# Windowed attention and routed experts on one core: row sums from a column of ones, copies moved to ScalarE, keys and queries laid out by group

## The chip, the core and the metric

The kernel runs on one core of a Trainium2 chip. A core has five engines with an instruction queue each, worked off in order: TensorE (PE in the profile; its weight loads are PEld), VectorE (DVE), ScalarE (ACT), GpSimd (POOL) and SyncE (SP), which here only issues transfers (DMA). Tiles lie in SBUF; PE writes into the eight banks of PSUM. The metric is the time of one execution on the device in microseconds (us): the median of several runs.

## What is computed

```python
B, H, S, D = 8, 8, 576, 64            # q, k, v: [B, H, S, D], fp32
scores = matmul(q, k.T) / 8           # per batch and head
rel = pos[:, None] - pos[None, :]
scores = where((rel >= 0) & (rel < 64), scores, -1e9)
attn = softmax(scores)
x = (attn @ v).transpose(0, 2, 1, 3).reshape(4608, 512)
logits = x @ w_gate + modality_bias[modality_id]      # 8 experts
e = argmax(logits, axis=1)
gate = softmax(logits)[e]
out[n] = gate[n] * (relu(x[n] @ w1[e]) @ w2[e])       # w1: 512x1024, w2: 1024x512 per expert
```

A query sees its own and the 63 keys before it. Each of the 4608 tokens goes through one expert.

## The kernel before

**Blocks and steps.** The sequence of each batch is cut in blocks of 64 positions, 72 in all; two neighbouring blocks are a pair `p`, 36 in all. A loop over steps `s` works in a pipeline: in step `s` the scores of pair `s` are computed, the probabilities of pair `s-1` are transposed, pair `s-2` is multiplied with its values, and pair `s-3` is routed. The order of each engine's queue is the order in which the loop emits its instructions. Two pairs are a group `G` of four blocks.

**One step, in the order of emission.** `values(s-2)` and `values_out(s-2)`: PE multiplies the transposed probabilities `pT` with the values, DVE multiplies the result by the reciprocals `rs` of the rows' sums into `xa`. `logits(s-3)` on PE and an addition on DVE into `lg`. `scores(s)`: 32 small PE matmuls into the two banks `sp`. `minima(s)`: eight custom DVE instructions add the mask and take each row's minimum of the negated scores (`ss`, `mn`). `swap_v(s-1)` and `probs_t(s-1)`. `exps(s)`: eight ACT instructions, in three portions, raise `e` to the shifted scores and sum each row into `sm`. `x_t(s-2)`: transposition for the logits. Then come two halves of the next group's heads: in an even step both halves of its keys, in an odd step both halves of its queries (`heads_t` on PE, `heads_out` on DVE or ACT). In odd steps from 5 on the routing of an older group (`route2`, `route3`) ends with an index `idx` on DVE and two scatters on POOL, which write rows `xa` to the scratch tensor `xs_scratch` in DRAM.

**Keys and queries.** `kT` and `qT` hold two groups, `[P, HP, RING, W64]`: head pair, then ring place of the block, then position; each group is a slice of four places in every head pair. Scores of a block read its own keys and those of the block ahead of it.

**Values.** `vo[p]` holds the pair's values by position. `ve[p]` holds the same two blocks shifted by one: its lower half is the lower half of `vo[p]` (copied by POOL), its upper half is the upper half of `vo[p-1]`, the neighbour (copied by DVE, `L502`). One matmul with `vo` and one with `ve` give a block its 128 keys.

**Experts.** The weights of two experts are loaded in pieces, split in a high and a low part (`Whi` on ACT, `Wlo` on DVE); a piece per step from step 3 on. From step `FIRST` = 12 on, the expert matmuls of rows scattered earlier fill gaps of the attention steps on PE; after step 39 they alone remain. `EARLY` fixes which groups' rows are taken when. Small DVE instructions that plan these loads stand in a queue of their own and are emitted a few at a time by `tick`.

**Banks.** `turn_bank` hands out banks for transposes in turn; up to step 10 there are five of them (two `tp`, `em`, `y0`, `y1`).

**The start.** Before step 0, SP and ACT issue the loads of group 0's keys and queries; ACT then issues those of the modality numbers (`mod_i`), the bias rows and the gate weights. `first_pair(0)` transposes and copies the first two blocks' heads; `first_pair(1)`, the other two blocks of group 0, follows the scores of step 0. A transposition of the modality numbers stands on PE between the heads of step 0 and the scores of step 1; from it POOL makes `bias_sel`.

## Time and profile before

| | |
|---|---|
| three runs | 647.55, 648.55, 649.33 us; median 648.55 |
| the profiled execution | 648.28 us, span 646.4 us |
| busy in the span | PE 620.0 us (96%), DVE 367.7 (57%), ACT 299.4 (46%), POOL 137.4 (21%) |
| granted clock of PE, mean | 0.996 |
| DMA | 88.07 MB, mean 136 GB/s; 116746 of 138885 packets under 512 B |
| minima of step 0 | start at 14.30 us |
| minima of step 12 | start at 86.23 us |

The span runs from the first to the last instruction; the profiled execution's time is 1.9 us longer. In a row of the timeline stand start, duration, engine, line of the kernel, instruction, tiles, shape, count, and in square brackets how long the engine sat idle ahead of it and what ended that. Instructions of one engine overlap, so the distance of two starts can be smaller than a duration. A row of the windows view gives, for a stretch, the busy time of each engine with its count of instructions, the granted clock of PE, the busy share of the 16 DMA engines and what they moved. A row of the waits view reads: who waited, for whom, us in total, times, the longest.

### The profile page before, as it was taken

The page shows a single profiled execution, that of the slowest core. Times are in us where ns is not written, and L with a number is a line of the kernel's source. Part 1 is how long each engine was busy: PE and PEld are TensorE (multiplying, and loading weights), DVE is VectorE, ACT ScalarE, POOL GpSimd, SP SyncE. Part 2 cuts the span into 40 slices and gives each one's busy share as a digit, 9 for nine tenths or more (in the row PEclk, how much of TensorE's full clock was granted, in tenths as well). Part 3 has the DMA queues.
Part 4 walks back from the last instruction along what each step waited for, and adds up shares of the span by engine and source line. Part 5 has one row for each costly group of instructions (what it writes and reads, how often), then busy time and mean ns, then how long its engine had stood idle before and what let it go on. Part 6 is the DMA issues. An engine that isn't in the chain of part 4 may idle for free.

```text
span 646.4 us, 17286 instructions
## 1 busy us (share of the span) xinstructions
PE 620.0 (96%) x6508; PEld 554.6 (86%) x6509; DVE 367.7 (57%) x1494; ACT 299.4 (46%) x932; POOL 137.4 (21%) x314
## 2 busy tenths in 40 slices
PE   6888889999999999999999999999999999999996
PEld 4677779898989888889998898899898999989986
DVE  2889967777767686766655365122214524757611
ACT  2789875756565646555544111111113513555411
POOL 4315330232142212320322220011011101101102
PEclk9999989999999999999999999999999999999999
DMA  9988975764876754553412124421041732677300
GB/s 164 195 186 216 212 197 132 196 161 120 181 171 153 159 144 103 144 133 82 132 51 83 50 99 171 157 67 66 23 173 45 236 113 85 218 247 227 120 1 36
DMA packets 138885, 88.07 MB, mean 136 GB/s; under 512 B 116746, under 2 KB 116784, under 8 KB 138672
## 3 DMA queue, kind: packets, MB, share of 16 engines
q1 hardware_dynamic: 130112, 67.44, 42.2%
q0 software_dynamic: 5856, 18.92, 7.8%
q10 hardware_dynamic: 2832, 0.59, 0.6%
q8 instruction: 52, 0.85, 0.6%
q14 instruction: 33, 0.27, 0.2%
HBM read 67.49 MB, written 23.91 MB: 141 GB/s over the span
## 4 chain that ended last, share of the span: by engine, by line
PE 50%; DVE 0%; ACT 0%; issue 0%; POOL 0%; POOLq 0%; ACTq 0%
PE y L301 22%; PE em L279 12%; PE sp L279 10%; PE tp L439 1%; PE y L352 1%; PE av L615 1%; PE em L254 1%; PE tp L254 1%; PE sp L327 0%; PE em L327 0%; PE tp L640 0%; PE sp L563 0%; DVE xa L623 0%; ACT ss L589 0%; DVE hl L288 0%
## 5 line engine op out<-in xcount | busy, mean ns | idle before, releaser
L301 PE MATMUL y<-Whi,hh 128*128 128x512 f32 x288 | 118.7, 412 | 0.0
L301 PE MATMUL y<-Wlo,hh 128*128 128x512 f32 x288 | 112.9, 392 | 0.0
L301 PE MATMUL y<-Whi,hl 128*128 128x512 f32 x288 | 112.8, 392 | 0.0
L589 ACT ACTIVATE ss<-ss,mn 128x128 f32<-128x128 f32 x288 | 112.5, 397 | 0.0
L279 PE MATMUL em<-xh,Whi 128*128 128x256 f32 x400 | 103.5, 293 | 1.2 <-ACT xh L192 0.7
L279 PE MATMUL em<-xh,Wlo 128*128 128x256 f32 x400 | 98.5, 280 | 0.0
L288 DVE SCALAR_TENSOR_TENSOR hl<-em,hh 128x512 fp32r<-128x512 f32 x50 | 34.5, 690 | 92.9 <-ACT hh L287 91.3
L312 POOL DMA_INDIRECT out_dram<-y,id x36 | 37.3, 1036 | 224.6 <-DVE y L309 145.9
L279 PEld LDWEIGHTS em<-xh,Whi 128*128 128x128 f32 x400 | 75.9, 190 | 2.6 <-ACT xh L192 0.9
L279 PEld LDWEIGHTS em<-xh,Wlo 128*128 128x128 f32 x400 | 75.8, 190 | 0.9
L287 ACT ACTIVATE hh<-em 128x512 fp32r<-128x512 f32 x50 | 29.6, 592 | 93.3 <-PE em L279 89.4
L577 DVE CUSTOM_DVE_ANT_0 ss<-sp,masks 128x128 f32<-128x128 f32 x288 | 63.5, 286 | 13.4 <-PE sp L563 13.4
L598 ACT COPY pT<-tp 128x512 f32<-128x512 f32 x58 | 32.2, 589 | 78.0 <-PE tp L439 78.0
L301 PEld LDWEIGHTS y<-Whi,hl 128*128 128x128 f32 x288 | 54.1, 188 | 12.3
L279 PE MATMUL em<-xl,Whi 128*128 128x256 f32 x400 | 63.4, 281 | 0.0
L301 PEld LDWEIGHTS y<-Whi,hh 128*128 128x128 f32 x288 | 54.1, 188 | 7.5
L301 PEld LDWEIGHTS y<-Wlo,hh 128*128 128x128 f32 x288 | 54.3, 188 | 7.1
L589 ACT ACTIVATION_READ_ACCUMULATOR ss<-ss,mn 128x1 f32 x288 | 55.8, 194 | 0.0
L716 POOL DMA_INDIRECT xs_scratch<-xa,idx x36 | 36.3, 1007 | 89.1 <-DVE lm L659 26.9
L279 PEld LDWEIGHTS em<-xl,Whi 128*128 128x128 f32 x400 | 54.2, 189 | 0.0
L288 DVE SCALAR_TENSOR_TENSOR hl<-sp,hh 128x512 fp32r<-128x512 f32 x22 | 15.2, 692 | 61.1 <-ACT hh L287 61.1
L615 PEld LDWEIGHTS av<-ve,pT 128*64 128x64 f32 x576 | 36.4, 138 | 15.2 <-issue 7.4
(242 smaller groups left out, 1243.6 us busy)
## 6 DMA issues: line engine op xcount, KB each, us to landing
xt<-xs_scratch SPq DMA_DIRECT2D x18, 514.0 KB, 4.0
vo<-in_v_dram SPq DMA_DIRECT2D x32, 256.0 KB, 4.1
y<-in_moe_w_dram SPq DMA_DIRECT2D x32, 256.0 KB, 4.0
vo<-in_moe_w_dram SPq DMA_DIRECT2D x24, 256.0 KB, 3.5
ss<-in_moe_w_dram SPq DMA_DIRECT2D x24, 256.0 KB, 3.8
qk<-in_k_dram SPq DMA_DIRECT2D x18, 256.0 KB, 5.5
qk<-in_q_dram SPq DMA_DIRECT2D x18, 256.0 KB, 4.9
xs_scratch<-xs_scratch SPq DMA_DIRECT2D x8, 514.0 KB, 6.0
```

The lines of the kernel that those rows point to most:

```text
L254: nc.tensor.transpose(out=tp[:, n * P:(n + 1) * P].bitcast(F32R), in_=xt[:, t, c * P:(c + 1) * P].bitcast(F32R), identity=ident_r)
L279: nc.tensor.matmul(out=hb[:, i * TP:(i + 1) * TP], lhsT=w[buf][:, c0:c0 + P], rhs=x[:, c * TP:(c + 1) * TP], start=(n == 0), stop=(n == le ...
L287: nc.scalar.activation(out=hh, in_=hb, func=AF.Relu),
L288: nc.vector.scalar_tensor_tensor(out=hl, in0=hb, scalar=0.0, in1=hh.bitcast(F32), op0=ALU.max, op1=ALU.subtract)))
L301: nc.tensor.matmul(out=sl["y", t], lhsT=h[:, i * TP + t * P:i * TP + (t + 1) * P], rhs=w[buf][:, c0:c0 + DM], start=(k == 0 and n == 0), s ...
L312: ins = nc.gpsimd.indirect_dma_start(out=out, out_offset=bass.IndirectOffsetOnAxis(ap=sl["id"][:, t:t + 1], axis=0), in_=y, in_offset=None ...
L352: nc.tensor.matmul(out=yp[:, cols], lhsT=sl["h", n][lo][:, c * P:(c + 1) * P], rhs=w[buf][:, c0 + cols.start:c0 + cols.stop], start=(m == ...
L577: nc.vector.tensor_tensor_reduce(out=ss[a][:, hp, :], in0=sp[a][:, hp * P:(hp + 1) * P], in1=mask, scale=-1.0 / 8.0, scalar=3.0e38, op0=AL ...
L589: nc.scalar.activation(out=ss[a][:, hp, :], in_=ss[a][:, hp, :], func=AF.Exp, bias=mn[:, h:h + 1], scale=-1.0, accum_out=sm[:, h:h + 1])
L598: nc.scalar.copy(out=pT, in_=pp)
L615: nc.tensor.matmul(out=av[c * W64:(c + 1) * W64, 2 * hp + a], lhsT=pT[:, i:i + W64], rhs=(vo if c else ve)[p][:, 2 * hp + a, :], start=Tru ...
L716: ins = nc.gpsimd.indirect_dma_start(out=xs, out_offset=bass.IndirectOffsetOnAxis(ap=idx[:, j:j + 1], axis=0), in_=xg[j], in_offset=None)
```

## The change

Six things change together.

1. Row sums. For pairs below `FIRST` the exponentials no longer sum their rows. `vo` and `ve` become fixed tiles with a 65th column per head that holds ones, and the values' matmul takes 65 columns; its last one is the row's sum. The result then needs two banks, `av` and `y1`, which leaves four for `turn_bank`. `values_out` adds 1e-9 on DVE (two instructions) where POOL did, and multiplies in two halves.
2. ScalarE copies. The neighbour's values in `ve` are copied by ACT for pairs below `FIRST`, at the start of a step (`swap_upper`); the second half of the queries' heads is copied by ACT in steps before `FIRST`.
3. `kT` and `qT` are laid out by group: group, head pair, place, position.
4. The first heads: transposes are ordered by the two loads they need (even and odd positions), and each copy of `first_pair(0)` is divided between DVE and ACT. `first_pair(1)` comes after five of step 0's exponentials, so on DVE after the minima. ACT issues the loads of modality numbers, bias rows and gate weights after the first copies.
5. The write of padding rows to `xs_scratch` (SP) moves from the end of step 2 to the end of step 5.
6. Two small tiles take the buffers of others (`wm` those of `lm`, `tgt` those of `wn`).

```diff
+    kT = att.tile([P, 2 * HP * GBLK, W64], F32, name="kT")
+    qT = att.tile([P, 2 * HP * GBLK, W64], F32, name="qT")
+    def place(g, hp):
+        a, j = divmod(g, GBLK)
+        return (a * HP + hp) * GBLK + j
+    vos = [att.tile([P, H, D + 1], F32, name=f"vo{i}") for i in range(3)]
+    ves = [att.tile([P, H, D + 1], F32, name=f"ve{i}") for i in range(2)]
...
-        if s < FIRST - 1 and i % 5 > 1:
-            return ps_m.tile([P, 512], F32, name=("em", "y0", "y1")[i % 5 - 2])
+        if s < FIRST - 1 and i % 4 > 1:
+            return ps_m.tile([P, 512], F32, name=("em", "y0")[i % 4 - 2])
...
-            nc.vector.tensor_copy(out=e[W64:P], in_=vo[p - 1][W64:P])
         nc.gpsimd.tensor_copy(out=e[0:W64], in_=vo[p][0:W64])
+    def swap_upper(p):
+        ve[p] = ves[p % 2]
+        if p > 0:
+            copy = nc.scalar.copy if p < FIRST else nc.vector.tensor_copy
+            copy(out=ve[p][W64:P], in_=vo[p - 1][W64:P])
...
-                bias=mn[:, h:h + 1], scale=-1.0, accum_out=sm[:, h:h + 1])
+                bias=mn[:, h:h + 1], scale=-1.0, accum_out=sm[:, h:h + 1] if p >= FIRST else None)
...
+        if p < FIRST:
+            for i in range(2):
+                nc.vector.tensor_scalar(
+                    out=rs[:, i * HP:(i + 1) * HP], in0=av[i][:, :, D], scalar1=1e-9, scalar2=None, op0=ALU.add)
         nc.vector.reciprocal(out=rs, in_=rs)
...
-    first_pair(0)
+    first_pair(0, (both, both))
+    nc.scalar.dma_start(out=mod_i, in_=mod_id.bitcast(I32).rearrange("(g x) -> g x", x=2 * P))
...
+        if 1 <= s <= NPR:
+            swap_upper(s - 1)
         if 2 <= s < NPR + 2:
             values(s - 2)
...
-                first_pair(1)
             minima(s)
...
+        if s == 0:
+            first_pair(1, (both[:1], both[1:]))
...
-            heads_out(tp, G, *heads[1], nc.scalar.copy if heads[1] == K1 else nc.vector.tensor_copy)
+            heads_out(tp, G, *heads[1], nc.scalar.copy if heads[1] == K1 or s < FIRST else nc.vector.tensor_copy)
...
-        if s == 2:
+        if s == 5:
             nc.sync.dma_start(out=xs_blk[DUMMY:DUMMY + 2].rearrange("b p c -> p b c"), in_=padrow)
```

How this moves instructions shows at three places. A row of these lists is one instruction in its engine's order: line, operation, output and inputs, shape, what its queue waits for, and a count where it is repeated. The first is ACT's queue from the last exponentials of step 5 to the probabilities' copies `pT` of step 6; before:

```order
L589 ACTIVATE ss,sm<-ss,mn 128x128 [waits DVE_49] x6
L111 CAST Whi_65<-y 128x512 [waits DMAHW1_49]
L598 COPY pT<-tp 128x512 [waits PE_49]
L598 COPY pT<-em 128x512 [waits PE_49]
L589 ACTIVATE ss,sm<-ss,mn 128x128 [waits DVE_49,Pool_49]
```

and of the change:

```order
L613 ACTIVATE ss<-ss,mn 128x128 [waits DVE_49] x6
L552 COPY qT<-em 128x2x2x128 [waits PE_49]
L111 CAST Whi_65<-y 128x512 [waits DMAHW0_49]
L517 COPY ve_111<-vo_108 64x520 [waits DMAHW2_49]
L622 COPY pT<-tp 128x512 [waits PE_49,Activation_49] x2
```

ACT has two copies more between the exponentials of an odd step and the `pT` of the next, and its exponentials write no `sm` and wait no longer for POOL.

The second is DVE at the end of an odd step; before, from the second half of the queries' heads to the addition of the logits:

```order
L539 COPY qT<-y_942 128x2x2x128 [waits PE_49]
L702 TENSOR_REDUCE se<-ex 128x2 [waits Activation_49]
L703 TENSOR_TENSOR tgt<-tgt,oh 128x16 [waits DVE_49]
L704 TENSOR_SCALAR se<-se 128x2 [waits DVE_49]
L706 TENSOR_REDUCE dst<-tgt 128x2 [waits DVE_49]
L710 RECIPROCAL xa_101<-se 128x1 [waits DVE_49]
L710 RECIPROCAL xa_102<-se 128x1
L728 CAST idx<-dst 128x2 [waits DVE_49]
L116 TENSOR_TENSOR Wlo_66<-y,Whi_65 128x512 [waits DMAHW0_49,Activation_49]
L621 RECIPROCAL rs<-rs 128x8 [waits Pool_49]
L623 TENSOR_TENSOR xa_105<-av,rs 128x512 [waits DVE_49,PE_49]
L645 TENSOR_TENSOR lg<-tp,bias_sel 128x8 [waits PE_49]
```

and of the change, where `wn` is the former `tgt`:

```order
L744 TENSOR_TENSOR wn<-wn,oh 128x16 [waits DVE_49]
L745 TENSOR_SCALAR se<-se 128x2 [waits DVE_49]
L747 TENSOR_REDUCE dst<-wn 128x2 [waits DVE_49]
L751 RECIPROCAL xa_101<-se 128x1 [waits DVE_49]
L751 RECIPROCAL xa_102<-se 128x1
L769 CAST idx<-dst 128x2 [waits DVE_49]
L116 TENSOR_TENSOR Wlo_66<-y,Whi_65 128x512 [waits DMAHW7_49,Activation_49]
L659 TENSOR_SCALAR rs<-av 128x4 [waits PE_49]
L659 TENSOR_SCALAR rs<-y_978 128x4 [waits PE_49]
L661 RECIPROCAL rs<-rs 128x8 [waits DVE_49]
L664 TENSOR_TENSOR xa_105<-av,rs 128x256 [waits DVE_49]
L664 TENSOR_TENSOR xa_105<-y_978,rs 128x256
```

The heads' copy has left DVE; the two instructions for `rs` and `xa` have become five.

The third is SP around the weights' piece and the values of step 6; before:

```order
L524 DMA Whi_64<-in_q_dram 64x8x64 [waits DMAHW5_49]
L100 ISA
L100 DMA y<-in_moe_w_dram 128x512 [waits DMAHW6_49]
L489 DMA vo<-in_v_dram 128x8x64 [waits DVE_49,DMAHW7_49,PE_49,Pool_49]
L104 ISA
```

and of the change:

```order
L538 DMA Whi_64<-in_q_dram 64x8x64 [waits DMAHW4_49]
L100 ISA
L100 DMA y<-in_moe_w_dram 128x512 [waits DMAHW5_49]
L1076 DMA xs_scratch<-xt 128x2x514 [waits DMAHW6_49,DMASW1_49,DMASW0_49]
L500 DMA vo_107<-in_v_dram 128x8x64 [waits PE_49,DMAHW7_49,Activation_49,Pool_49]
```

The write of the padding rows stands ahead of `vo` and waits for the two scatters of group 0 (`DMASW0`, `DMASW1`).

More of the change, by code (lines that the diff above doesn't have):

```diff
@@ L695, in route3 @@
         xg = [st.pop((GB * G + j, "xa")) for j in range(GB)]
-        tgt = small.tile(sh3, F32, name="tgt")
+        tgt = small.tile(sh3, F32, name="wn")
         nc.vector.tensor_tensor(
@@ L860, in tile_window_attn_moe @@
                     pattern=[[1, W64]], channel_multiplier=-1)
+    for t in vos + ves:
+        nc.gpsimd.memset(t[:, :, D:], 1.0)
     nc.gpsimd.memset(first_oh, 0.0)
@@ L926, in select_bias, with first_pair @@
                 nc.gpsimd.tensor_tensor(out=bias_sel, in0=bias_sel, in1=dst, op=ALU.add)
-    def first_pair(i):
-        for nm in "kq":
-            first_heads(nm, i, turn_bank(0), nc.vector.tensor_copy if nm == "k" else nc.scalar.copy)
-    first_pair(0)
+    both = nc.vector.tensor_copy, nc.scalar.copy
+    def first_pair(i, copies):
+        tps = [turn_bank(0) for _ in "kq"]
+        for t in range(2):
+            for nm, tp in zip("kq", tps):
+                first_heads_t(nm, i, t, tp)
+        for nm, tp, c in zip("kq", tps, copies):
+            first_heads_out(nm, i, tp, c)
+    first_pair(0, (both, both))
+    nc.scalar.dma_start(out=mod_i, in_=mod_id.bitcast(I32).rearrange("(g x) -> g x", x=2 * P))
+    nc.scalar.dma_start(
+        out=brow, in_=mod_bias.rearrange("(o m) e -> o m e", o=1).broadcast_to([P, 2, E]))
+    nc.scalar.dma_start(out=wg, in_=w_gate.rearrange("(c p) e -> p c e", p=P))
     def weights(s):
```

95 lines of the change are left out of this document (55 added, 40 removed).

## The prediction

> **What bounds the kernel now.** I read the busy time of each engine by stretch first, because shares over the whole span (PE 96%) mix stages with different limits. I cut the stretches at the starts of DVE's score minima (`L577`), which mark the attention steps.
>
> ```profile
> core 0: us, PE busy (x) PEld busy (x) DVE busy (x) ACT busy (x) POOL busy (x), PEclk, DMA share, GB/s
> ...
> 14.30:25.31 11.01, 8.36 (x129) 6.25 (x127) 8.28 (x53) 8.87 (x38) 5.43 (x11) 1.00 1.19 203
> ...
> 48.73:72.19 23.46, 20.75 (x410) 18.35 (x408) 22.53 (x122) 21.90 (x85) 9.20 (x17) 1.00 0.88 212
> 72.19:86.23 14.04, 10.45 (x200) 8.62 (x199) 12.65 (x74) 10.72 (x42) 4.36 (x9) 1.00 0.76 180
> 86.23:100.00 13.77, 11.82 (x143) 10.66 (x142) 8.95 (x45) 8.56 (x28) 4.87 (x10) 0.88 0.92 229
> 100.00:627.00 527.00, 525.23 (x5075) 474.32 (x5074) 288.72 (x1084) 224.69 (x656) 98.33 (x206) 1.00 0.46 129
> ```
>
> From 100 us on PE is busy 525.23 of 527.00 us. Nothing that the change takes from DVE or ACT can count there; PE's work there stays. The change can only move the whole of it forward, by making steps 0 to 11 end earlier. In the four steps from 48.73 to 72.19 DVE is busy 22.53 of 23.46 us (96%), ACT 93%, PE 88%: DVE sets the pace, ACT is just behind it. So the second view is DVE's timeline over one odd step (minima of step 7 to minima of step 8); the columns are start, duration, instruction.
>
> ```profile
> 54.67 0.28 DVE L577 CUSTOM_DVE_ANT_0 ss<-sp,masks 128x128 f32<-128x128 f32 x1
> ...
> 56.47 0.42 DVE L502 COPY ve<-vo 64x512 f32<-64x512 f32 x1
> 56.93 0.69 DVE L539 COPY qT<-tp 128x512 f32<-128x512 f32 x1
> ...
> 57.74 0.68 DVE L539 COPY qT<-em 128x512 f32<-128x512 f32 x1
> 58.34 0.16 DVE L702 TENSOR_REDUCE se<-ex 128x2 f32<-128x16 f32 x1
> ...
> 59.54 0.20 DVE L621 RECIPROCAL rs<-rs 128x8 f32<-128x8 f32 x1
> 59.82 0.69 DVE L623 TENSOR_TENSOR xa<-av,rs 128x512 f32<-128x512 f32 x1
> 60.43 0.15 DVE L645 TENSOR_TENSOR lg<-y,bias_sel 128x8 f32<-128x8 f32 x1
> 60.50 0.28 DVE L577 CUSTOM_DVE_ANT_0 ss<-sp,masks 128x128 f32<-128x128 f32 x1
> ```
>
> No row carries an idle mark: DVE goes from one instruction to the next. Durations overlap, so I price an instruction by start to start: the neighbours' copy `ve` 0.46 us, a heads' copy 0.60 (57.74 to 58.34), `xa` 0.61, the dependent step from `rs` to `xa` 0.28. Earlier steps do have waits, and the waits view gives their sum:
>
> ```profile
> DVE ss L577 <- PE sp L563: 5.3, 6, 2.2
> 42.88 0.29 DVE L577 CUSTOM_DVE_ANT_0 ss<-sp,masks 128x128 f32<-128x128 f32 x1 [1.25 <-PE sp L563]
> 42.27 0.45 PE L563 MATMUL sp<-kT,qT 64*64 64x128 f32 x8 [0.97 <-ACT kT L539]
> 48.73 0.28 DVE L577 CUSTOM_DVE_ANT_0 ss<-sp,masks 128x128 f32<-128x128 f32 x1
> ```
>
> The scores of step 5 wait at 42.27 for ACT's key copy, though that copy writes the next group's places in `kT`; DVE waits behind them. The old layout interleaves both groups in one run of addresses, and the wait comes from that.
>
> **The change, part by part.** (1) DVE per step. Each step to 11 loses `ve` (−0.46); each odd one also its second heads' copy (−0.60). Added is the split `values_out`: two small additions, one more dependent step and a second multiplication. The additions follow each other like `lg` and the next instruction (60.43, 60.50: 0.07); the step from addition to reciprocal I bound by 0.07 (no dependence) and 0.28 (`rs` to `xa`) and take 0.2, the dependent end; two halves of `xa` instead of one add one start, 0.07 again. Together about +0.35 per step. Even steps: −0.1. Odd steps: −0.7.
>
> (2) ACT per step. The exponentials lose their accumulator reads; the price is not the read's own 0.2 us:
>
> ```profile
> 49.06 0.59 ACT L598 COPY pT<-em 128x512 f32<-128x512 f32 x1
> 49.54 0.41 ACT L589 ACTIVATE ss<-ss,mn 128x128 f32<-128x128 f32 x1
> 49.85 0.20 ACT L589 ACTIVATION_READ_ACCUMULATOR ss<-ss,mn 128x1 f32 x1
> 49.94 0.40 ACT L589 ACTIVATE ss<-ss,mn 128x128 f32<-128x128 f32 x1
> ...
> 53.22 0.62 ACT L539 COPY kT<-tp 128x512 f32<-128x512 f32 x1
> 53.73 0.62 ACT L111 CAST Whi<-y 128x512 fp32r<-128x512 f32 x1
> ```
>
> A pair takes 0.40 start to start; the read starts 0.31 after its ACTIVATE. Without the read the next can start there, so one saves 0.09 and eight 0.7. ACT gains the neighbours' copy and, in odd steps, a heads' copy, each like `kT`: 0.51. Even steps −0.2, odd +0.3. By these rows (8 × 0.40; two `pT` and, taken as equal, one `xaT` at 0.48, from 49.06 to 49.54; one `Whi` at 0.51) an odd step holds 5.15 us of ACT work and goes to 5.45. So odd steps cannot shrink from 5.83 (54.67 to 60.50) to DVE's 5.1, only to about 5.45: −0.4. That is the take-over I count on: ACT becomes the bound of odd steps. Even steps stay with DVE, whose 5.7 is above ACT's 5.55.
>
> (3) Steps 2 to 10: five even at −0.1 and four odd at −0.4 is −2.1. The false wait ahead of step 5's minima, 1.25, goes with the layout (true keys were written a step earlier); DVE's other waits in steps 3 to 10 are small, and I leave them. Sum −3.4. Steps 10 and 11 (72.19 to 86.23) carry extra planning instructions on DVE; for step 11 I count nothing, since the first expert rows, which come after the plan, are wanted at once in step 12.
>
> (4) The start. The second half of the first heads (`first_pair(1)`) moves on DVE from before the minima of step 0 to behind them, the first heads are transposed in order of arrival and copied by both engines, and step 1's scores no longer wait for the next group's key copy.
>
> ```profile
> 3.99 0.59 ACTq L820 DMA_DIRECT2D y<-in_moe_modality_id_dram  x1
> 8.74 0.61 ACT L551 COPY qT<-tp 128x512 f32<-128x512 f32 x1 [3.63 <-PE tp L439]
> 18.46 0.45 PE L563 MATMUL sp<-kT,qT 64*64 64x128 f32 x8 [1.07 <-ACT kT L539]
> 18.97 0.29 DVE L577 CUSTOM_DVE_ANT_0 ss<-sp,masks 128x128 f32<-128x128 f32 x1 [2.20 <-PE sp L563]
> 10.20 0.29 POOL L912 CAST y<-y 36x128 f32<-36x128 int32 x1 [1.05 <-DMA y<-in_moe_modality_id_dram]
> 16.86 0.33 POOL L920 TENSOR_SCALAR y<-y 128x36 f32<-128x36 f32 x1 [6.37 <-DVE y L916]
> 20.51 0.60 POOL L503 COPY ve<-vo 64x512 f32<-64x512 f32 x1
> ```
>
> DVE's wait of 2.20 before step 1 goes (upper end: with it also part of the 1.07, some 3). Against it: the modality numbers are asked for behind the first copies on ACT, at about 9.3 (8.74 + 0.61) instead of 3.99; they reached POOL at 10.20 and would come at about 15, and PE has their transposition in its queue ahead of step 1's scores. Their chain on POOL takes 4.3 us to the first `ve` (16.86 to 21.11), ahead of the first values. Lower end: the gain is 1.0. I take −2.1, nearer to the wait that is seen. The five memsets of the ones' columns on POOL sit in its slack before 10.20 (1.05 idle).
>
> (5) The write of the padding rows moves from step 2 to the end of step 5, and there it stands behind the first scatter: it writes the same scratch, so SP waits until both scatters of group 0 have landed, with `vo` of step 6 in the queue behind it.
>
> ```profile
> 45.27 0.39 SPq L489 DMA_DIRECT2D vo<-in_v_dram  x1
> 47.10 0.15 DVE L728 CAST idx<-dst 128x2 int32<-128x2 f32 x1
> 49.89 0.97 POOL L716 DMA_INDIRECT xs_scratch<-xa,idx  x1 [0.28 <-POOL xa L715]
> DMA to landing us min/median/max: 3.7/4.1/4.5
> 23.21 1.11 SPq L1024 DMA_DIRECT2D xs_scratch<-xt  x1
> 57.04 0.24 PE L615 MATMUL av<-ve,pT 128*64 128x64 f32 x1
> 58.62 1.10 PE L563 MATMUL sp<-kT,qT 64*64 64x128 f32 x32
> vo<-in_v_dram SPq DMA_DIRECT2D x6, 256.0 KB, 4.0
> ```
>
> (The landing times are those of the writes to the scratch up to 56 us.) Count from the minima of step 6, at 48.73. `vo` of step 6 is issued 3.5 us before that now. After: the second scatter starts 1.16 after it (49.89), less the 0.35 by which `values_out` pushes the minima; with 4.1 it has landed at +4.9. Then the padding's issue, 0.4 to 1.1; `vo` lands 4.0 later, or some 1.2 more behind the padding's 514 KB; POOL's copy is 0.6. So the values of step 8 can start at +9.9 to +11.8. They start at +8.3 now (57.04); step 8's scores are done 2.7 later (59.72), and DVE takes them at 60.50, +11.8, or +11.3 with steps 6 and 7 shortened. So DVE needs the values begun by +8.6. A stall of 1.3 to 3.2, once; I take the middle, 2.2. The keys for step 8, issued behind it, are wanted later in that step and hide in the same stall. In exchange the start loses 514 KB and 1.11 us of SP's time at 23.21, where nobody was waiting.
>
> (6) Costed at nothing: 65 columns for 64 in the values of 12 steps (PE is at 88% there), one bank fewer for transposes (a bank is free again when ACT or DVE has copied it, four uses back; if ACT falls behind, PE waits, and that is in the next figure), the renamed small buffers (all on DVE, in order). For engines that now run closer together I add 0.6 of new small waits, between none and 1.2, three odd steps' gain.
>
> Sum: −3.4 −2.1 +2.2 +0.6 = −2.7. The profiled execution took 648.28 us (span 646.4 and 1.9 around it), 0.27 below the median of 648.55. 648.28 − 2.7 = 645.6.
>
> **Rivals.** (a) The padding's wait hides: scatters land sooner, or values have more slack. For it: DMA has less to do while SP waits. Then 645.6 − 2.2 = 643.4. Chance 0.19.
>
> (b) The start gives nothing: the modality numbers come after 16 and hold PE and the POOL chain. For it: DMA's share is 1.19 up to 25.31, so a later request queues. 645.6 + 2.1 = 647.7, no measurable change. Chance 0.13.
>
> (c) The clock. The granted clock is 0.88 between 86.23 and 100, a loss of 13.77 × 0.12 = 1.7 us, behind the stretch in which PE was busiest least (10.45 of 14.04). A new gap at step 8 could bring a second such drop: 645.6 + 1.7 = 647.3, chance 0.06; a better fed PE could lose the one there is: 643.9, chance 0.08. [...]
>
> (d) Slower: DMA becomes the bound. Rows of `vo` now lie 65 values apart, so its pieces of 256 bytes land at uneven addresses. DMA's share is 0.88 with 212 GB/s in steps 6 to 9, that is some 1.24 MB per step, of which `vo` is 0.26, a fifth. [...] Against it: nothing in the trace writes such pieces. Chance 0.07. [...]
>
> **How the numbers follow.** The forecast, 645.6 with its own range 643.7 to 647.5 (both ends of the stall and of the start), has 0.47, four fifths of it below 646.6. (a) has 0.19, (b) 0.13, (c) 0.14, (d) 0.07. About 0.3% (1.9 us) is what a measurement of this kernel can tell from no change, so faster means below 646.6: 0.38 of the forecast, (a), the drop that goes (0.08) and 0.05 of (b) and the second drop, 0.70. Slower is (d) and 0.01 of bad cases together, 0.08; the same is what is left, 0.22. The range reaches down past (a), with the larger start, to 641.7, and up past (b) to 648.2; outside stay (d) and some 0.1 of the rest.
>
> **What would show it.** Minima of step 1 near 16.8 instead of 18.97 and no `kT` wait ahead of the scores; odd steps shorter by about 0.4 and even ones unchanged, with ACT, no longer DVE, the busier engine in odd ones; SP's row for the padding near 50 with `vo` right behind it, and POOL or PE waiting for `vo` in step 7 or 8; the stretch from step 12 on as long as before. The forecast is wrong if step 8 shows no gap, if step 1's scores wait for the modality numbers, or if landing times of `vo` rise well above 4.0.

## The result, and the profile after

The change made the kernel slower: it took 651.81 us in the median of six runs (648.26 to 655.75), against 648.23 (647.24 to 649.33) for six runs of the kernel before beside them. The ratio is 1.0053, with a 95% interval of 1.0028 to 1.0078. Forecast were 645.6 us, and 648.2 as the upper end. The profiled execution took 649.57 us, with a span of 647.7.

The windows of the kernel after, at the cuts that the prediction used (columns: stretch, its length, busy us of PE, PEld, DVE, ACT and POOL, granted clock, DMA share, GB/s):

```profile
14.30:25.31 11.01, 9.32 (x191) 8.44 (x195) 9.55 (x59) 8.90 (x25) 4.91 (x9) 1.00 1.09 198
...
48.73:72.19 23.46, 20.34 (x403) 17.84 (x397) 19.55 (x123) 22.32 (x57) 7.76 (x14) 1.00 1.09 253
72.19:86.23 14.04, 11.67 (x156) 9.81 (x155) 10.01 (x67) 9.87 (x26) 3.61 (x7) 0.76 1.02 234
86.23:100.00 13.77, 11.30 (x149) 10.18 (x148) 8.96 (x36) 9.48 (x33) 1.40 (x3) 1.00 0.54 123
100.00:627.00 527.00, 522.05 (x5047) 470.59 (x5046) 284.80 (x1075) 221.91 (x646) 98.16 (x206) 1.00 0.45 129
```

Three things stand in these rows. In the second row ACT is the engine that is nearly always busy (22.32 of 23.46 us) and DVE has fallen from 22.53 to 19.55: the take-over happened. In the third the granted clock is 0.76: two stretches of 3.41 us at half speed (77.0 to 83.8), where the kernel before had one, later (91.6 to 95.0). And in the last row, where the prediction said that nothing could change, PE is busy 522.05 us and not 525.23. PE idles 3.2 us more in steps that the change seemed not to concern.

The start did better than forecast, and the false wait is gone. Step 1's minima start at 15.54 (before 18.97), step 5's at 37.82 (before 42.88), 5.1 us earlier. Step 12's start at 84.07 (before 86.23): of the lead, 2.9 us are lost again in steps 5 to 11. Steps 5 to 9 lose 1.3 of them (30.59 us, before 29.31). Steps 10 and 11 lose 1.6, and step 11 holds both half-speed stretches, which cost up to 3.4.

The timelines of steps 5 and 7 show how the first part is lost: first PE's scores and DVE's minima of step 6, then DVE, ACT, POOL and PE of step 7.

```profile
43.79 0.67 PE L587 MATMUL sp<-kT,qT 64*64 64x128 f32 x16 [0.69 <-ACT qT L552]
44.51 0.29 DVE L601 CUSTOM_DVE_ANT_0 ss<-sp,masks 128x128 f32<-128x128 f32 x1 [1.09 <-PE sp L587]
...
50.31 0.62 ACT L517 COPY ve<-vo 64x520 f32<-64x520 f32 x1
50.95 0.58 ACT L622 COPY pT<-em 128x512 f32<-128x512 f32 x1
51.44 0.59 ACT L622 COPY pT<-y 128x512 f32<-128x512 f32 x1
52.05 0.69 ACT L613 ACTIVATE ss<-ss,mn 128x128 f32<-128x128 f32 x2
...
53.34 0.61 POOL L511 COPY ve<-vo 64x520 f32<-64x520 f32 x1 [8.19 <-DMA vo<-in_v_dram]
54.00 0.27 PE L649 MATMUL av<-ve,pT 128*64 128x65 f32 x1 [1.27 <-POOL ve L511]
54.97 0.16 DVE L659 TENSOR_SCALAR rs<-av 128x4 f32<-128x4 f32 x1 [1.65 <-PE av L649]
```

DVE, which had no idle marks in the step that the prediction shows, now waits (1.09, 1.65). Behind the first wait stands ACT: the queries' copy comes after all of ACT's exponentials of the step, the next scores need it, and the minima need the scores. Behind the second stands POOL, whose copy into `ve` the values need. POOL's wait of 8.19 is the padding write's: SP issued it at 48.26 and `vo` at 48.83, after both scatters had landed, as the prediction said.

The late idle is in the waits from 100 to 627 us. PE's waits for the bank of the logits, before and after:

```profile
PE tp L439 <- DVE lg L645: 1.3, 3, 0.7
```

```profile
PE tp L439 <- DVE lg L686: 4.2, 5, 1.3
```

One of the five, in DVE's and PE's timeline of a step of the expert stage after the change:

```profile
182.66 0.43 DVE L517 COPY ve<-vo 64x520 f32<-64x520 f32 x1
183.12 0.20 DVE L661 RECIPROCAL rs<-rs 128x8 f32<-128x8 f32 x1
183.41 0.69 DVE L664 TENSOR_TENSOR xa<-av,rs 128x512 f32<-128x512 f32 x1
184.02 0.16 DVE L686 TENSOR_TENSOR lg<-tp,bias_sel 128x8 f32<-128x8 f32 x1
...
184.23 0.66 PE L439 MATMUL tp<-ident_r,ss 128*128 128x128 f32 x4 [0.71 <-DVE lg L686]
```

`swap_upper` is called at the start of every step. For pairs from `FIRST` on it still copies on DVE, but now ahead of `rs`, `xa` and `lg`; the copy takes 0.46 from start to start. `lg` frees the bank `tp` that PE needs next, and PE has nothing else in its order there. In the kernel before the copy stood behind the minima (as in the odd step that the prediction shows, at 56.47), and `lg` came that much sooner.

### The profile page after: what moved, and what is told of

Its sections match the earlier page's. It is cut to its first block, busy times and chain, and to the rows that moved or that the text cites. A ratio compares the mean times of both kernels' runs of the same rounds, so it can differ in the third digit from the quotient of the medians.

```text
span 647.7 us, 17192 instructions
## 1 busy us (share of the span) xinstructions
PE 620.6 (96%) x6509; PEld 554.9 (86%) x6509; DVE 361.6 (56%) x1514; ACT 302.0 (47%) x854; POOL 133.0 (21%) x307
## 5 line engine op out<-in xcount | busy, mean ns | idle before, releaser
L613 ACT ACTIVATE ss<-ss,mn 128x128 f32<-128x128 f32 x288 | 105.9, 394 | 2.8 <-DVE mn L601 2.5
L622 ACT COPY pT<-tp 128x512 f32<-128x512 f32 x61 | 34.2, 588 | 83.3 <-PE tp L439 83.2
L301 PEld LDWEIGHTS y<-Wlo,hh 128*128 128x128 f32 x288 | 54.3, 188 | 7.1
L287 ACT ACTIVATE hh<-sp 128x512 fp32r<-128x512 f32 x22 | 13.1, 597 | 76.6 <-PE sp L279 76.6
L587 PE MATMUL sp<-kT,qT 64*64 64x128 f32 x1152 | 42.2, 284 | 2.3 <-ACT qT L552 1.7
```

Source lines behind the costliest of these rows:

```text
L287: nc.scalar.activation(out=hh, in_=hb, func=AF.Relu),
L301: nc.tensor.matmul(out=sl["y", t], lhsT=h[:, i * TP + t * P:i * TP + (t + 1) * P], rhs=w[buf][:, c0:c0 + DM], start=(k == 0 and n == 0), s ...
L587: nc.tensor.matmul(out=sp[a][c * W64:(c + 1) * W64, hp * P:(hp + 1) * P], lhsT=qT[rows, place(g + c, hp), :], rhs=kT[rows, win(c, hp), :], ...
L613: nc.scalar.activation(out=ss[a][:, hp, :], in_=ss[a][:, hp, :], func=AF.Exp, bias=mn[:, h:h + 1], scale=-1.0, accum_out=sm[:, h:h + 1] if ...
L622: nc.scalar.copy(out=pT, in_=pp)
```

## The experiments

All ratios are to runs of the kernel before beside them on the same chip. "1 to 12" is the time from step 1's minima to step 12's in the profiled execution, "rest" that from step 12's minima to the span's end; both less 1.7 us (half its length, an estimate) for each stretch of 3.41 us at half speed that lies in them; a stretch across step 12's start is shared out by its parts.

| kernel | ratio (95%) | median us | step 1 at | 1 to 12 | rest |
|---|---|---|---|---|---|
| before | 1 | 648.2 to 649.6 | 18.97 | 67.3 | 558.5 |
| after | 1.0053 (1.0028 to 1.0078) | 651.81 | 15.54 | 65.1 | 563.6 |
| e1_late | 1.0010 (0.9987 to 1.0032) | 649.39 | 15.69 | 69.0 | 559.4 |
| e2_pad | 1.0023 (0.9998 to 1.0048) | 651.16 | 17.73 | 67.4 | 564.3 |
| e3_copies | 1.0032 (1.0017 to 1.0048) | 652.23 | 17.87 | 72.3 | 557.3 |
| e4_acc | 1.0125 (1.0096 to 1.0154) | 658.59 | 17.50 | 69.9 | 562.8 |
| e5_q_pad | 0.9996 (0.9975 to 1.0018) | 648.86 | 15.72 | 66.2 | 559.4 |
| e6_dve_pad | 1.0006 (0.9988 to 1.0025) | 649.72 | 18.07 | 69.0 | 558.2 |
| e7_start | 0.9947 (0.9928 to 0.9967) | 645.05 | 17.94 | 67.1 | 558.2 |
| e8_late_pad | 0.9946 (0.9927 to 0.9965) | 645.81 | 17.55 | 64.9 | 558.9 |
| e9_w0 | 0.9908 (0.9887 to 0.9928) | 642.79 | 15.30 | 65.0 | 559.3 |
| e10_w12 | 0.9897 (0.9878 to 0.9915) | 641.95 | 17.41 | 64.6 | 559.4 |
| e11_w_both | 0.9891 (0.9873 to 0.9910) | 641.66 | 15.60 | 65.0 | 559.5 |
| e12_after_w | 1.0004 (0.9988 to 1.0020) | 648.67 | 17.49 | 65.2 | 563.4 |
| f1_pad5 | 0.9976 (0.9962 to 0.9989) | 645.97 | 14.72 | 67.7 | 559.6 |
| f2_late | 1.0012 (0.9997 to 1.0026) | 648.68 | 17.93 | 67.8 | 563.9 |
| f3_no12 | 0.9933 (0.9913 to 0.9952) | 644.14 | 17.40 | 66.9 | 558.2 |
| f4_q | 0.9947 (0.9922 to 0.9971) | 644.61 | 15.22 | 68.4 | 559.4 |
| g1_only_late | 1.0072 (1.0046 to 1.0097) | 653.89 | 18.96 | 67.9 | 562.1 |
| g2_before_w12 | 0.9986 (0.9969 to 1.0003) | 648.12 | 19.21 | 68.0 | 558.4 |

e5 to e8 ran side by side on one chip, e9 to e12 side by side on that chip at another time; e1 to e4, f1 to f4 and the two g each side by side on a chip of their own. A difference of ratios between two of these groups is less sure than one within a group.

### The late copy: e1_late, f2_late, g1_only_late

```diff
     def swap_v(p):
...
+        if p >= FIRST:
+            nc.vector.tensor_copy(out=e[W64:P], in_=vo[p - 1][W64:P])
...
     def swap_upper(p):
...
-        if p > 0:
-            copy = nc.scalar.copy if p < FIRST else nc.vector.tensor_copy
-            copy(out=ve[p][W64:P], in_=vo[p - 1][W64:P])
+        if 0 < p < FIRST:
+            nc.scalar.copy(out=ve[p][W64:P], in_=vo[p - 1][W64:P])
```

That is e1_late. f2_late is the reverse on the best kernel (e11_w_both), and g1_only_late puts the copy at the step's start in the kernel before, with no other edit.

> The changed kernel with one line of part 2 undone: for pairs from 12 on the neighbours' copy ve stands on DVE again behind the minima, where it stood before the change, not at the start of the step. Theory 1 (the moved DVE copy stands ahead of rs, xa and lg, so the bank that the logits hold comes free 0.44 us later and PE waits for it): from 100 to 627 us PE is busy about 525.2 instead of 522.05, PE's waits tp <- DVE lg fall from 4.2 to about 1.3 us, and the median falls by 3, from 651.8 to about 648.8; step 12's minima stay at 84.1. Rival (the late idle comes from the layout by group or the renamed small buffers): PE's busy time there stays near 522 and the median moves by less than 1. Second rival (the loss is half-speed windows in steps 10 to 13): the late idle goes but the median stays above 650.

> The kernel of ratio 0.9891 with the ve copy of pairs from 12 on at the start of the step, as in the change. Theory: PE busy 522.05 instead of 525.1 from 100 to 627 us, +3.2 us, ratio 0.994. Rival (PE's late idle is caught up at the end): ratio below 0.992.

> The kernel before with one edit of the change and nothing else: for pairs from 12 on DVE's ve copy stands at the start of the step, ahead of rs, xa and lg. Theory (this one copy is the late loss): step 12's minima at 86.2 as before, PE busy 522 instead of 525.2 from 100 to 627 us, from step 12's minima to the end 562 to 564 us where the kernel before has 558.5 without its half-speed window; ratio 1.005 to 1.007. Rival (the late loss needs the change's other parts beside it): PE busy 525, ratio within 0.002 of 1.

The windows from 100 us on and PE's waits for the logits' bank there, of e1_late, then of g1_only_late:

```profile
100.00:627.00 527.00, 525.27 (x5071) 474.09 (x5070) 288.79 (x1078) 223.53 (x652) 97.99 (x206) 1.00 0.45 129
PE tp L439 <- DVE lg L687: 1.3, 3, 0.7
```

```profile
100.00:627.00 527.00, 522.04 (x5058) 471.18 (x5057) 285.81 (x1087) 223.82 (x654) 97.43 (x206) 1.00 0.46 129
PE tp L439 <- DVE lg L648: 4.2, 5, 1.3
```

With the copy back in its place PE is busy 525.27 again; with that one copy moved in the kernel before it is busy 522.04, and the whole kernel comes out at 1.0072, slower than the full change. In every kernel of the table with the late copy the rest takes 562.1 to 564.3 us, in every one without it 557.3 to 559.6. This shows the cause of the late loss: one DVE copy of 0.46 us a step, ahead of the instruction that frees a bank. In the kernel before it costs 3.6 us in the profile (562.1 less 558.5) and 4.7 by the ratio; in the changed kernel it costs 4.2 (after and e1_late) or 4.4 (f2_late and e11_w_both) in the profile. By the ratios of pairs that differ in this copy alone but ran on two chips it is less sure: from 1.8 us (e12_after_w and f1_pad5) to 7.8 (f2_late and e11_w_both). f2_late came out at 1.0012 where 0.994 was expected; its rest grew by 4.4 us as it should, but its steps 1 to 12 took 2.8 longer than in e11_w_both, which this copy does not touch (see what stays open, below).

### Sums and copies: e3_copies, e4_acc, e6_dve_pad, e7_start, f3_no12, e5_q_pad, f4_q

e3_copies undoes part 2 (both copies on DVE, in the old places). e4_acc undoes part 1:

```diff
-                ... accum_out=sm[:, h:h + 1] if p >= FIRST else None)
+                ... accum_out=sm[:, h:h + 1])
-        if p >= FIRST:
+        if True:
             nc.gpsimd.tensor_scalar(out=rs, in0=sm, ...)
```

with the values in one bank and five banks for transposes again. e6_dve_pad is e3_copies with the padding write back at step 2; e7_start undoes parts 1, 2 and 5, so parts 3, 4 and 6 are left; f3_no12 is e7_start with the fillers told of below. e5_q_pad and f4_q move only the second heads' copy of odd steps back to DVE, without and with fillers (late copy and padding are in their old places in both).

> The changed kernel with part 2 undone: the neighbours' copies and the second heads' copies are on DVE in their old places, in all steps. Theory (ACT is the bound of steps 5 to 10: 5.8 us of work per step with the added copies 0.64 and 0.50): without them ACT holds 5.2 per step and DVE becomes the bound with its old work and the split values_out, 0.35 more: steps of 6.1 to 6.3, evenly, no pairs of 6.7 and 5.1; step 12's minima between 82 and 85, the late idle gone as in the run before, median 646.5 to 649.5. Rival (the copies on ACT are a gain, and only the later steps cost): step 12's minima come later than 85.5 and the median is above 649.5.

> The changed kernel with part 1 undone (sums by the exponentials' accumulators, POOL's addition, values in one bank, five banks for transposes; the tiles stay 65 wide). Theory (ACT is the bound): its exponentials take 0.39 instead of 0.30 start to start, 0.75 more per step, so steps 5 to 10 get longer by up to 0.7 each, step 12's minima come 3 to 5 later than 84.1, median 654 to 657. Rival (DVE with the split values_out is the bound): steps get shorter by 0.35, step 12's minima near 82, median about 649.7.

> Parts 3, 4 and 6 alone (layout by group, the first heads, the renamed buffers); parts 1, 2 and 5 undone, tiles of the values still 65 wide. By the prediction's steps: start -2.1, the wait of 1.25 ahead of step 5's minima gone, later steps as before: step 12's minima at 82.5 to 84 (before 86.23), PE busy 525 from 100 us on, median 3 below the kernel before, ratio 0.995. Rival (how far the start gains hangs on when PE leaves its half rate at the start: matmuls ahead of step 1 run at half rate up to 12.1 in one profile and 16.9 in another): step 1's minima at 17.5 to 18 in this profile and a gain of 1.3 only, ratio 0.997. Second rival: the layout's wait comes back elsewhere and the ratio is 1.

> The kernel of ratio 0.9891 with parts 1 and 2 undone: sums by the accumulators, both copies on DVE, five banks; parts 3, 4 and 6 and the fillers stay. Theory (parts 1 and 2 only trade ACT's time against DVE's and are worth nothing in steps 2 to 10; 47.5 us in them before and after, without the wait of step 5): step 12's minima within 1 us of the other kernel's once the time of step 1 is taken off (65.0 us), ratio 0.988 to 0.991. Rival (they are worth the 2.1 us of the prediction): ratio 0.9923.

Part 1 and part 2 hang on each other. Without part 2, DVE carries the split `values_out` as well as its copies: e6_dve_pad 1.0006 against e8_late_pad 0.9946, side by side. Without part 1, ACT carries the accumulators as well as the copies: 1.0125, though not all of this is ACT's work, for four half-speed stretches lie in that profile. The theory for e3_copies (ACT the bound, so DVE copies would help) fell. But together they are worth nothing: e7_start without both 0.9947, e8_late_pad with both 0.9946. The windows of steps 5 to 9 and of steps 10 and 11, of f3_no12 (without parts 1 and 2), then e11_w_both (with them):

```profile
40.28:69.62 29.34, 26.05 (x518) 23.64 (x516) 28.20 (x151) 28.09 (x108) 10.01 (x19) 1.00 0.83 194
69.62:84.32 14.70, 12.61 (x214) 9.89 (x212) 12.74 (x74) 10.73 (x42) 4.94 (x10) 1.00 0.88 212
```

```profile
37.49:67.73 30.24, 26.26 (x511) 22.93 (x510) 25.16 (x157) 29.41 (x75) 9.72 (x16) 1.00 0.97 216
67.73:80.58 12.85, 12.11 (x211) 9.90 (x213) 11.81 (x74) 11.87 (x30) 2.50 (x6) 1.00 0.86 214
```

DVE is relieved of 3.0 us in steps 5 to 9, ACT gets 1.3 more and is busy 97%; the five steps take 0.9 us longer, where the forecast was 1.4 less (three odd steps at −0.4, two even at −0.1). What the pair of parts wins is in steps 1 to 4 (1.0 between these two profiles) and in steps 10 and 11 (1.85, where DVE also has the planning), and 1.3 is lost in the rest, 0.6 of it in step 12 (11.42 us against 10.79); why was not traced. f3_no12's ratio of 0.9933 lies above e11_w_both's by 0.0042, 2.7 us, a little more than the rival said, but on another chip; and of the 2.4 us between the two profiles 1.8 lie ahead of step 1 (17.40 against 15.60), where the pair does nothing. So the pair is worth nothing by the comparison side by side, whose intervals leave 1 to 2 us either way, and 2.7 us at most.

> The changed kernel with the late ve copy back behind the minima, the padding write back at step 2, and the second heads' copy of odd steps back on DVE; the neighbours' copy ve stays on ACT in steps below 12. Theory (ACT sets the pace of steps 5 to 10 because it holds both copies: 34.5 us of work in 35.6 over six steps): ACT loses 0.5 per odd step and PE's next scores no longer wait for ACT's qT (waits of 1.7 us), DVE's odd step becomes 5.7; steps 5 to 10 average 5.9 instead of 6.2, and from step 1 to step 12 it takes 65 to 66 us less half-speed windows (now 68.5 with two of them, 1.7 each); PE busy 525 from 100 us on; median 2 below the kernel with the late copy alone, a ratio to before of about 0.998. Rival (that copy on ACT costs nothing): the steps stay at 6.2 and the ratio at 1.001.

> The kernel of ratio 0.9891 with the second heads' copy of odd steps on DVE again. Theory (ACT holds 5.75 us of work a step and sets the pace; without this copy 5.25 in odd steps): odd steps 5, 7 and 9 fall from 6.6 to about 5.5 and even ones rise to 5.3, steps 5 to 10 take 36.0 instead of 36.9; ratio 0.988. Rival (its ratio of 0.9996 without fillers was the steps and not the clock): ratio 0.994 or above.

These two do not decide. From step 5's minima to step 10's the same code took 29.35 us in e5_q_pad's profile and 32.17 in f4_q's; by the ratios the copy is better on ACT, as the rival said (0.9996 against e8_late_pad's 0.9946 side by side, 0.9947 against e11_w_both's 0.9891 on two chips), though one of the two profiles has the short steps that the theory expected. More on the longer steps stands under what stays open.

### The padding write: e2_pad, e6_dve_pad, e8_late_pad, f1_pad5

```diff
-        if s == 5:
+        if s == 2:
             nc.sync.dma_start(out=xs_blk[DUMMY:DUMMY + 2]..., in_=padrow)
```

> The changed kernel with part 5 undone: the padding write is at the end of step 2 again. If SP's wait for the scatters holds step 7: vo of step 6 lands some 6 us earlier, POOL's wait of 8.19 for it goes, PE's gap of 1.27 ahead of the values at 54.0 goes, step 7 (7.01 us) falls to about 6.0, and step 12's minima come about 1 earlier than 84.1; median about 650.8. If ACT sets the pace of the pair of steps 7 and 8 anyway (12.36 us, of which ACT is busy all but 0.65): step 7 gets shorter by at most 0.65 and the median moves by less than 1. The start may lose up to 1.1 (SP's time for the write).

> The changed kernel with parts 2 and 5 undone (both copies on DVE in all steps, padding write at step 2). The run with part 2 alone undone had one step 7 of 8.41 us with PE waiting 2.11 ahead of the values. Theory (that step is the padding's wait, free of ACT's cover): step 7 falls to 6.1, PE's wait there goes, steps 5 to 10 average 6.2, step 12's minima come 2.3 earlier, 88 without a second half-speed window; ratio to before about 0.999. Rival (the wait there is not the padding's): step 7 stays above 7.5.

> The changed kernel with the late ve copy back behind the minima and the padding write back at step 2. Theory (while ACT sets the pace, the padding's wait of step 7 hides mostly): step 7 stays at 6.7 to 7.1, the ratio to before is that of the late copy alone, 1.001, or 0.001 lower. Rival (the padding costs its 2.2 us in full): ratio 0.9975.

> The kernel of ratio 0.9891 (late copy and padding in their old places, both fillers) with the padding write at the end of step 5 again. Theory (most of its wait hides behind ACT's queue, and the 4 us between the ratios 1.0010 and 0.9946 were clock windows): step 7 rises from 6.61 to 7.0 or 7.2, later steps stay, +0.5 us, ratio 0.989 to 0.991. Rival (the stall of 2.2 us of the prediction is there in full): ratio 0.9925 or above.

Where ACT does not cover it, the wait is what the prediction said. SP's queue, POOL's copy and PE's values of step 7 in e3_copies (padding at step 5, copies on DVE):

```profile
52.53 0.40 SPq L1075 DMA_DIRECT2D xs_scratch<-xt  x1
53.10 0.39 SPq L500 DMA_DIRECT2D vo<-in_v_dram  x1
...
57.30 0.61 POOL L513 COPY ve<-vo 64x520 f32<-64x520 f32 x1 [6.55 <-DMA vo<-in_v_dram]
57.97 0.27 PE L648 MATMUL av<-ve,pT 128*64 128x65 f32 x1 [2.11 <-DVE wn L743]
```

The label names DVE, but the values start when POOL's copy into `ve` ends, and that copy waited for `vo`. With the write at step 2 the wait goes: step 7 takes 8.41 us in e3_copies and 6.45 in e6_dve_pad, 1.96 less, although a half-speed stretch reaches 1.4 us into the latter. In kernels with the copies on ACT the profiles show far less: step 7 takes 7.01 in the change and 6.90 in e2_pad, although POOL's wait for that `vo` falls from 8.19 to 2.11; it takes 7.16 (e1_late) and 6.84 (e8_late_pad), 6.86 (e12_after_w) and 6.61 (e11_w_both). Yet the ratios of e1_late and e8_late_pad differ by 0.006, those of f1_pad5 and e11_w_both by 0.0085, each pair on two chips; with the late copy present the padding is worth 0.003 (after and e2_pad) or nothing (e12_after_w and f2_late). e8_late_pad and f1_pad5 so went against the theory that ACT hides the wait, without a profile that shows where all of the time goes. The clock is a part of it: the mean over e1_late's runs is 0.993 and over e8_late_pad's 0.995, as an estimate 1.6 of the 4.1 us between them. The padding's price by the ratios lies between 0 and 5.5 us, and its size in the whole change is not settled; the forecast of 2.2 is inside.

### The clock: e9_w0, e10_w12, e11_w_both, e12_after_w, g2_before_w12

The runs of the change lie 7.5 us apart, and the mean granted clock goes with them (0.995 at 648.26, 0.988 at 655.75): 0.007 of 648 us is 4.5 of the 7.5. The price of one half-speed stretch can be read from the 120 runs of the kernel before that stand beside the experiments: in each of the five groups those with a mean clock of 0.998 or more are shorter by 1.2 to 2.4 us (medians) than those with 0.994 to 0.996. The windows of the kernel after around its half-speed stretches, one before and two within:

```profile
73.60:77.00 3.40, 1.59 (x13) 1.17 (x12) 3.32 (x24) 2.72 (x7) 0.00 (x0) 1.00 1.10 213
77.00:80.40 3.40, 2.84 (x30) 2.15 (x28) 2.35 (x13) 3.40 (x11) 0.65 (x1) 0.50 0.64 125
80.40:83.80 3.40, 3.40 (x66) 3.22 (x64) 1.35 (x6) 0.82 (x2) 2.35 (x6) 0.50 1.07 335
```

and of the kernel before, one before and one within:

```profile
88.15:91.56 3.41, 1.54 (x10) 0.96 (x9) 2.35 (x6) 3.41 (x13) 1.86 (x5) 1.00 1.21 296
91.56:94.97 3.41, 3.33 (x15) 3.33 (x16) 1.95 (x7) 1.67 (x9) 0.77 (x1) 0.50 0.77 211
```

In these two profiles a stretch in which PE is busy 45 to 47% is followed by 3.41 us at half speed. Over all profiles the stretch ahead of such a drop has PE busy 40% (e8_late_pad, 75.03 to 78.45) to 60% (e4_acc, 71.40 to 74.81), in 13 cases. (The expectation of e10_w12 below has 42 and 53% for the two drops of e8_late_pad; over the full stretches it is 40 and 55.) No sharp limit comes out of this: a stretch with 50% (e6_dve_pad, 79.48 to 82.89) and one with 54% (e7_start, 75.75 to 79.16) are followed by full speed. The start has a half rate of its own, which the clock's column (1.00 there) doesn't show. The same eight transposes ahead of step 1, in the kernel after and in e2_pad:

```profile
13.18 1.09 PE L439 MATMUL tp<-ident_r,Whi 128*128 128x128 f32 x8
```

```profile
14.02 1.97 PE L439 MATMUL tp<-ident_r,Whi 128*128 128x128 f32 x8
```

PE's start-of-kernel matmuls go to full rate at 12.1 us in the one and at 16.9 in the other. The traces' records of the clock begin only there (12.16 and 17.04 us), so the column's 1.00 ahead of that stands for a stretch without a record. The later changes of the clock lie whole multiples of 3.413 us after this first one or after each other (in the kernel before 78.507 us, 23 of them, to the drop, and 549.546 us, 161 of them, from its end to the next). The fillers are matmuls on zeros into a bank that holds nothing at the time, placed where PE waits:

```diff
-    WARM = 4, 3
+    WARM = 7, 3
+            if i == 0:
+                keep_warm(1)          # behind each set of first transposes (e9_w0)
...
+            if s == FIRST - 1:
+                keep_warm(5, "y0")    # behind the scores of step 11 (e10_w12)
+        if s in (FIRST - 1, FIRST):
+            keep_warm(3 if s == FIRST else 1, "y0")   # ahead of the first heads; 2 behind them
```

e9_w0 has the first set, e10_w12 the second, e11_w_both both, all on e8_late_pad; e12_after_w is the change as it is with both; g2_before_w12 is the kernel before with the second.

> The kernel with the late ve copy and the padding back in their old places (ratio 0.9946), plus matmuls on zeros that fill PE's idle time at the start: seven instead of four at the beginning and one behind each of the two sets of first transposes. In ten profiles PE's matmuls of the start leave half rate at 12.1 to 13.0 or at 16.6 to 17.3, once at 20.0. Theory (half rate ends after a stretch of some 3.4 us in which PE was busy enough, so the idle 1.76, 0.64 and 0.61 ahead of step 0's scores decide): full rate from 9 to 13 us in this profile, step 1's minima at 15.7 or sooner instead of 17.5 to 18, no slow executions for that reason, the ratio 0.002 to 0.003 lower. Rival (the time of the change of rate hangs on something else): step 1's minima at 17.5 still, and the ratio as before or higher by the 0.3 us that late fillers cost.

> The kernel of ratio 0.9946 plus matmuls on zeros where PE idles in steps 11 and 12: five behind the scores of step 11, one and two around its first heads, three and two around those of step 12. Theory (the granted clock halves for 3.41 us after a stretch of that length in which PE is busy for less than about half: 42% ahead of the drop at 78.4, 53% ahead of that at 92.0): no half-speed window between 75 and 100 in this profile, the mean clock of all runs rises from 0.995 to 0.998, and the ratio falls by 0.002 to 0.003. Rival (drops don't hang on PE's busy share): windows at half speed stay as many, and the fillers cost up to 1 us: ratio 0.996.

> Both sets of fillers of the two runs before it on the kernel of ratio 0.9946. Theory: both gains add, ratio 0.989 to 0.991, about 642 us, mean clock 0.998, spread of the runs below 3 us. Rival (fillers do nothing): 0.995.

> The changed kernel as it is, with both sets of fillers and nothing else. It tells how much of its 0.5% loss is clock: its runs had a mean clock of 0.992 (a loss of 5.2 us, where the kernel before loses 2.0 to 2.9), and its start leaves half rate early in some executions only. Theory: of the +3.5 us, the late idle of 3.2 and most of the padding's wait stay, the clock's share of 2 to 3 goes and the start gains 1 to 2 in the mean: ratio 0.998 to 1.001. Rival (clock differences are an effect of the later work and not a loss by themselves): ratio 1.004 or above.

> The kernel before with the fillers of steps 11 and 12 alone. Theory (its runs lose one half-speed window in steps 12 and 13 in most executions): no window between 75 and 100 in this profile, ratio 0.996 to 0.9975. Rival (the fillers helped the other kernel only because it reaches step 12 sooner and idles longer there): ratio 0.999 or above.

The windows of e11_w_both, same cuts as above:

```profile
72.19:86.23 14.04, 12.36 (x158) 8.88 (x150) 11.47 (x67) 12.68 (x36) 3.90 (x9) 1.00 0.98 232
86.23:100.00 13.77, 13.65 (x166) 12.49 (x166) 9.74 (x42) 9.85 (x34) 1.91 (x4) 1.00 0.61 138
```

No half speed is left there, and the ratio falls from 0.9946 to 0.9891, the fastest kernel of this study, 6.7 us below the kernel before beside it; its runs lie within 1.2 us. Each set alone gives most of this (0.9908 and 0.9897), so the gains do not add as the theory said. Not all of it is clock: the mean over e9_w0's runs is 0.995 as in e8_late_pad, but in its profile step 1 starts 2.3 us sooner and steps 5 to 9 take 30.2 us for 31.4. With both sets, one profile reached full rate at 12.5 us and e12_after_w's only at about 17, so the start's fillers do not decide when the rate changes; their separate gain is not shown. In the profiles of the kernels before and after, PE is busy 3.13 and 3.35 us in the 3.41 us ahead of this change, and 2.05 and 1.96 in the 3.42 ahead of those; that such a stretch ends the half rate, as e9_w0's theory has it, no run shows. In the change as it is, fillers are worth 1.0053 to 1.0004. In the kernel before the half-speed stretch goes too, but only 0.9986 is gained (0.9969 to 1.0003; expected 0.9975 or less): steps 1 to 12 took 0.7 longer, nearly all of it in step 11 (7.61 us, before 6.96), as in g1_only_late, which has no fillers.

So the change lost more to the clock than the kernel before. The mean clock is 0.992 over its runs and 0.997 over the 120 of the kernel before, as an estimate 5 us against 2. What makes the slack differs: ahead of the drop in the change's profile PE waits 1.57 us for DVE's `lg` (at 75.39), with DVE busy 3.32 of 3.40 us, and in e8_late_pad's 1.9 us for ACT's `pT`.

## Why the prediction was wrong, point by point

Two steps failed: the late steps, whose time the prediction held to be fixed, and the gain of parts 1 and 2. Beside them the sum has no term for the clock, which stands only as rival (c).

In the profiled execution the account closes: −3.4 us ahead of step 1, −1.6 in steps 1 to 4, +1.3 in steps 5 to 9, +1.6 in steps 10 and 11 (with two half-speed stretches) and +3.5 from step 12 on (where the kernel before has its one half-speed stretch) make +1.3 before rounding, which is what the span grew by. By the ratios it is: the late copy, never counted, +4.7 (g1_only_late); parts 1 and 2, forecast at −2.1, 0 (e7_start against e8_late_pad); parts 3 and 4, forecast at −1.25 and −2.1, together −3.4 (e7_start); the padding, forecast at +2.2, +1.9 by e2_pad (0 to 5.5 by the others). The sum is +3.2; 0.0053 of 648 is 3.4. Each of these terms holds its share of half-speed stretches, and with other pairs of ratios the late copy and the padding come out otherwise, so that the second sum comes out so near is in part luck.

- **"Nothing that the change takes from DVE or ACT can count there."** This first step failed. It is right of work that is taken away, and it was used as if nothing were moved there. The diff has DVE's copy for pairs from `FIRST` on in `swap_upper`, ahead of `values_out`, and the prediction priced the ve copy only up to step 11. PE at 525.23 of 527.00 us is not a sign of slack that protects: it says that any wait there counts in full. The prediction expected the time from step 12 on to stay as before; less half-speed stretches it grew from 558.5 to 563.6 us, 3.6 to 4.4 of that by this copy. Some 1 us more stands there in every kernel in which ACT copies `ve` in the early steps (558.9 to 559.6 with the late copy in its old place, against 557.3 to 558.5 where DVE does); its cause was not traced.
- **(1), DVE per step.** Right, and a little more: 3.0 us less DVE work in steps 5 to 9 (f3_no12 against e11_w_both), where three odd and two even steps make 2.3 by the forecast. It was worth nothing, because of the next step.
- **(2), ACT per step.** The direction was right (ACT becomes the bound), the size was not. Summed from start to start over six steps, from the first exponentials of step 5 on and without idle time, ACT's work is 34.2 us, 5.70 a step; before it was 32.8, 5.46. Forecast was +0.05 a step, measured +0.24. The exponentials save what was forecast (0.39 to 0.30 each); but `ve` holds ACT for 0.64 (50.31 to 50.95) and not 0.51, and a `pT` ahead of the exponentials for 0.61 (51.44 to 52.05) and not 0.48. A price read from a copy with another successor does not carry over. (The 5.55 that the prediction gives for even steps is 5.47 by its own rows, 5.15 and a second `kT` at 0.51 less 0.19; its conclusion would be the same.)
- **(3), steps 2 to 10.** The false wait ahead of step 5's minima went with the layout: step 4 takes 4.8 to 5.2 us in every kernel with it, 6.35 before (36.53 to 42.88). The −2.1 of steps 2 to 10 did not come: with the wait they were to take 3.4 us less, and took 0.8 less (53.16, before 53.96).
- **(4), the start.** Right, and modality numbers hold nothing: POOL has them at 12.78 and step 1's minima start at 15.54, −3.4, when PE reaches full rate early; at 17.4 to 18.1, −0.9 to −1.6, when it doesn't. That e7_start's −3.4 is the forecast of parts 3 and 4 is in part luck: in its profile 1.0 is won ahead of step 1, 0.2 in steps 1 to 12, where step 4 wins 1.2 and steps 8 and 11 lose it again, 0.3 behind, and 1.7 because the half-speed stretch of the kernel before is missing.
- **(5), the padding.** The mechanism was right to the row; 1.96 us of step 7 where DVE is the bound, 0.1 to 0.3 where ACT covers it. The 1.2 us for the padding's 514 KB were an estimate; at the 391 GB/s that the kernel before moved from 25.30 to 26.50 us, with this write under way, they would be 1.3. In the change `vo` behind it came 4.5 us after its issue (48.83 to 53.34, where POOL's copy starts), between the 4.0 and the 5.2 of the forecast.
- **(6).** Nothing was seen of its own. ACT's queries' copy ahead of the next scores (three times, 1.7 us in all) is a new small wait of the kind counted.
- **The rivals.** (a) and (b) did not happen alone. (c) did: a second half-speed stretch in the profiled execution, and more in others. Of PE's 1.95 us of idle time between 86.23 and 100 in the kernel before, 1.87 lay in the one stretch of 3.41 ahead of the drop. (d) is refuted: e7_start and e8_late_pad keep `vo` 65 wide and are 0.5% faster, and between 14 and 70 us its transfers land after 4.7 us (median) before and after. Nor is a DMA share of 1.0 a limit: the rows show 1.19 before and 1.09 after.

What stays open: steps 5 to 9 took 30.2 to 30.6 us in some profiles of kernels with the copies on ACT and 31.4 to 32.4 in others, with the same code in those steps (e8_late_pad 31.4, e10_w12 30.3, on one chip). In the longer ones DVE and ACT wait for PE at places where PE's records show it as done, as here in f4_q, where the rows of these scores end at 54.31:

```profile
56.70 0.29 DVE L602 CUSTOM_DVE_ANT_0 ss<-sp,masks 128x128 f32<-128x128 f32 x1 [1.76 <-PE tp L439]
```

The trace's records of the semaphores, by which engines signal each other, tell a little more: PE's signals stop at 53.30 and come again from 56.68 on, ten of them within 0.4 us, though the rows of their matmuls end between 54.3 and 56.2. In e8_late_pad they pause for 3.22 us in the same step (55.30 to 58.52), in e10_w12 for 1.96 at most in steps 5 to 9. So the engines behind waited for PE's signals. Why these came late, or whether the rows are early, was not found.

## What to carry to other kernels

A helper that is called in every step moves work in every step: read a moved line for each stage it runs in, and in a stage where one engine is busy 99% of the time ask what every moved instruction stands ahead of there. When work goes from the busiest engine to the one just behind it, price it by start to start with its real neighbours: the second engine was 0.4 us a step behind and became the bound at once. Where an engine's clock falls after a slack stretch (here to 0.50 for 3.41 us, behind stretches with PE busy 40 to 60%), idle time is paid twice, and cheap filler work in known waits can help (here 18 matmuls, 3.6 us in one kernel); in the kernel before, 13 of them gained 0.9 us, which is not clear of noise.
